# Attention with a mixture of experts on one core: when the first early expert's weights are loaded and split, and two banks at a time in its first layer

## The chip, the core and the metric

The kernel runs on one core of a Trainium2 chip. The metric is the device time of one execution in microseconds, the median of several runs. A profile is one execution recorded by the hardware profiler. The core's engines are PE (matrix products, with PEld loading their weights), DVE, ACT and POOL (vector work), and SP, whose queue issues nearly all plain transfers here.

## What is computed

Block-sparse attention over 4 batches, 8 heads, 768 tokens of width 64: in blocks of 32 tokens, each query block sees itself and its neighbours, the first and last block, and three drawn blocks; the first and last query block see all. Its output, 3072 tokens of width 512, goes through a mixture of 8 experts: a gate picks one expert for each token, and that expert's two layers are applied.

```python
scores = np.where(mask, scale * np.matmul(q, k.transpose(0, 1, 3, 2)), -1e9)
attn = softmax(scores); x = (attn @ v) as [3072, 512]
logits = x @ w_gate + modality_bias[modality_id]
e_idx = np.argmax(logits, axis=1)
for e in range(8):
    h = np.maximum(x[mask_e] @ w1[e], 0.0)        # w1[e]: 512 x 1024
    out[mask_e] = gate_w[mask_e] * (h @ w2[e])    # w2[e]: 1024 x 512
```

## The kernel before

**Attention.** The work is a list of items in a fixed order. Each pass of the main loop is one tick: it takes the next item and, for items begun some ticks earlier, the next step. The steps of a sparse item are S (scores, PE line 537), M (mask and row minimum, DVE line 545), X (exponentials, ACT line 553), T (transposes of X's result, PE line 562, in the same tick as X), A (copy of T's result out of its bank, ACT line 567), W and V (products with the values, PE lines 584 and 593), O (division, DVE lines 445 to 447), Y (transposes of the finished rows, PE line 600, copied by ACT at 602) and G (gate, PE line 610). Four items make one tile of 128 query rows. A tile's own values come through SP in six pieces of 128 KB (`fetch_own`, line 525), three at a time, and two more at lines 499 and 500; keys are picked by POOL (line 485), shared values copied by POOL (line 507), the queries loaded at line 148, finished rows stored at line 335. `hook(place)` is called at places 0 to 7 of a tick, and runs side work there: place 3 stands before the tick's S, place 7 at its end.

**Experts.** Tokens are sorted into groups of 256 that share an expert. Two groups (0 and 1) are formed early, from the experts that have enough tokens before attention is over; `early_groups` is a generator that is stepped once a tick at the place that `EARLY` gives. Group 0 belongs to the first early expert. An expert's weights are eight chunks of 512 KB: chunks 0 to 3 from w1, 4 to 7 from w2; chunks are counted on over the groups. `fetch(n)` (lines 717 and 721) has SP load chunk n into the staging buffer `staged(n)`. `split(n)` makes two halves of it: a rounded one by a cast on ACT (line 725) and the remainder by a subtraction (line 729) on DVE, or on POOL in four parts for the chunks in `POOL_SPLITS` (1, 2 and 4 among them). A staging buffer can be loaded again when both halves are made. `load(nf, ns)` fetches and splits in turn until chunk nf is fetched and chunk ns split. Its calls in the attention ticks are set by a counter of ticks:

```python
p = sum(tick >= x for x in TICKS)      # TICKS = (6, 9, 12)
load(p + 2, p)
```

So chunks 0 and 1 are fetched at the counter's tick 0, and at ticks 6, 9 and 12 one is split and another fetched into the buffer that this frees. `tail[0]` turns true some ticks after the last item has begun; then `expert_slots` takes over further buffers, and the first layer of group 0 begins.

**First layer.** `up(g, c, f, o)` (lines 777 to 779) makes three products of chunk c into column part f of a bank; two parts f fill a bank, and a bank needs all four chunks. `relu` (ACT line 784, DVE line 785) takes a full bank out. Each `yield` lets remaining attention and routing steps in between. The second layer is `down` (lines 792 to 794), fed by chunks 4 to 7. `column` (PE line 766, ACT 770, DVE 771) turns gathered tokens. After the two early groups, all other groups follow with PE near its limit.

Every engine works in the order in which the code issues to it, so what is issued earlier on an engine or a queue stands ahead of what comes later, and holds it back while it waits.

Of the kernel before, what the change touches and what calls it, by code (L numbers as in the profile page):

```python
# [62 lines left out]
LHS = (6, 5)  # L63
LHS_DVE = (True, True)
CHOOSE = ((0, 2),)
EARLY = ((3, 3),)

KL = (0, 3)
QP = (-2, 2)
# [10 lines left out]
EVAC_DVE = ()  # L80
POOL_SPLITS = (1, 2, 4, 7, 15, 16, 21)

TICKS = (6, 9, 12)
DOWN0 = ((9, 5), (9, 7), (14, 7), (12, 9), (13, 9), (13, 9), (17, 9), (15, 10))
UP1 = ((13, 8), (13, 14), (17, 15), (20, 15))
DOWN1 = ((16, 17), (17, 16), (17, 17), (23, 18), (21, 17), (23, 18), (23, 19), (22, 19))
# [3 lines left out]
def attention_moe(ctx, tc, kD, qD, qH, v0, v1, blocks, modality, w_gate, bias, w1, w2, out):  # L90
# [33 lines left out]
    with ExitStack() as actx:  # L124
# [5 lines left out]
        def bank():  # L130
            return psum.tile([P, 512], F32, name="bank")
# [522 lines left out]
        stg, wh, wl, xg, xh, xl, hh, hl, og, xq = [], [], [], [], [], [], [], [], [], []  # L654
# [41 lines left out]
        NSTG, NRING, LOOK_D, LOOK_S = 5, 5, 6, 4  # L696
# [7 lines left out]
            return experts[g]  # L704

        def staged(n):
            return stg[(0, 1, 0, 1, 0, 1, 0, 2)[n] if n < 8 else n % NSTG]

        def fetch(n):
            g, c = divmod(n, 8)  # L710
            e = expert(g)
            if c < 4:
                if g < FIRST_Q:
                    src = w1[bass.ds(e, 1), c * P:(c + 1) * P, :].rearrange("e p f -> p (e f)")
                else:
                    src = w1[bass.ds(e, 1)].rearrange("e (p c) f -> c p (e f)", c=4)[c]
                nc.sync.dma_start(staged(n), src)
            else:
                c -= 4
                src = w2[bass.ds(e, 1), 2 * c * P:(2 * c + 2) * P, :].rearrange("e (k p) f -> p (e k) f", p=P)  # L720
                nc.sync.dma_start(staged(n).rearrange("p (k f) -> p k f", k=2), src)

        def split(n, eng=None):
            h, l = wh[n % NRING], wl[n % NRING]
            nc.scalar.copy(h, staged(n))  # L725
            eng = eng or (nc.gpsimd if n in POOL_SPLITS else nc.vector)
            size = 256 if eng is nc.gpsimd else 1024
            for k in range(0, 1024, size):
                eng.tensor_tensor(l[:, k:k + size], staged(n)[:, k:k + size], h[:, k:k + size].bitcast(F32), ALU.subtract)  # L729

        def gather(g):
            ix = gi_e[g] if g < NEAR else gi[:, 2 * g:2 * g + 2]
            for t in range(2):
                nc.gpsimd.indirect_dma_start(
                    out=xg[2 * (g % 2) + t], out_offset=None, in_=x_d[0:TES[g] * P] if g < NEAR else x_d,
                    in_offset=bass.IndirectOffsetOnAxis(ap=ix[:, t:t + 1], axis=0))
# [26 lines left out]
        def column(g, n, xp):  # L763
            for c in range(2):
                for t in range(2):
                    nc.tensor.transpose(xp[:, c * GT + t * P:c * GT + (t + 1) * P],
                                        xg[2 * (g % 2) + t][:, (2 * n + c) * P:(2 * n + c + 1) * P], ident)
            h = xh[g % 2][:, 2 * n:2 * n + 2, :].rearrange("p a b -> p (a b)")
            l = xl[g % 2][:, 2 * n:2 * n + 2, :].rearrange("p a b -> p (a b)")
            nc.scalar.copy(h, xp)  # L770
            nc.vector.tensor_tensor(l, xp, h.bitcast(F32), ALU.subtract)

        def up(g, c, f, o):
            h, l = wh[(8 * g + c) % NRING], wl[(8 * g + c) % NRING]
            o = o[:, (f % 2) * GT:(f % 2 + 1) * GT]
            fs = slice(f * P, (f + 1) * P)
            nc.tensor.matmul(o, lhsT=h[:, fs], rhs=xh[g % 2][:, c, :], start=c == 0 and f % 2 == 0, stop=False)  # L777
            nc.tensor.matmul(o, lhsT=h[:, fs], rhs=xl[g % 2][:, c, :], start=False, stop=False)  # L778
            nc.tensor.matmul(o, lhsT=l[:, fs], rhs=xh[g % 2][:, c, :], start=False, stop=c == 3 and f % 2 == 1)  # L779

        def relu(k, o):
            rh = hh[0][:, 2 * k:2 * k + 2, :].rearrange("p a b -> p (a b)")
            rl = hl[k // 2][:, k % 2 * 2:k % 2 * 2 + 2, :].rearrange("p a b -> p (a b)")
            nc.scalar.activation(rh, o, AF.Relu)  # L784
            nc.vector.scalar_tensor_tensor(rl, o, 0.0, rh.bitcast(F32), ALU.max, ALU.subtract)  # L785
# [18 lines left out]
        def early_groups():  # L804
            now = {"fetch": 0, "split": 0, "gather": 0, "column": 0}

            def load(nf, ns):
                while True:
                    f, p = now["fetch"], now["split"]
                    if p < ns and p < f:  # L810
                        split(p)
                        now["split"] += 1
                    elif f < nf and f - NSTG < p and (f < 8 * NEAR or known):
                        fetch(f)
                        now["fetch"] += 1
                    else:
                        return

            def rows(g):
                if now["gather"] == g and ready[g] and (g != 1 or tail[1]):  # L820
                    if g == 1:
                        expert_slots(8)
                    gather(g)
                    now["gather"] += 1

            def columns(g):
                for n in range(2):
                    if now["column"] == 2 * g + n and now["gather"] > g:
                        column(g, n, bank())
                        now["column"] += 1  # L830
                        return

            expert_slots(0)
            tick, wait = 0, 0
            while not tail[0]:
                rows(0)
                if now["gather"]:
                    wait += 1
                    if wait > 4:
                        columns(0)  # L840
                p = sum(tick >= x for x in TICKS)
                load(p + 2, p)
                tick += 1
                yield "tick"
            expert_slots(2, 5, 6, 7)
            while now["column"] < 2:
                rows(0)
                columns(0)
            load(10, 5)
            for k in range(4):  # L850
                o = bank()
                for c in range(4):
                    for f in (2 * k, 2 * k + 1):
                        up(0, c, f, o)
                    rows(1)
                    yield
                relu(k, o)
            o = [bank() for _ in range(2)]
            for f in range(8):
                load(*DOWN0[f])  # L860
                for t in range(2):
                    down(0, f, t, o[t])
                    rows(1)
                    yield
                if f in (3, 7):
                    columns(1)
            while not tail[1]:
                yield
            rows(1)
            for t in range(2):  # L870
                give(0, t, o[t])
            while now["column"] < 4:
                columns(1)
            o = [bank() for _ in range(4)]
            for c in range(4):
                load(*UP1[c])
                for f in range(8):
                    up(1, c, f, o[f // 2])
                    if f % 2:
                        rows(2)  # L880
                        yield
            for k in range(4):
                relu(k, o[k])
            o = [bank() for _ in range(2)]
            for f in range(8):
                load(*DOWN1[f])
                for t in range(2):
                    down(1, f, t, o[t])
                    rows(2)
                    yield  # L890
                if f in (5, 6):
                    columns(2)
            for t in range(2):
                give(1, t, o[t])
            while not ready[2]:
                yield
            rows(2)
            load(22, 17)
            while now["column"] < 6:
                columns(2)  # L900
            piece_numbers(bank())
            load(22, 20)
# [128 lines left out]
        def choose(i):  # L1031
# [19 lines left out]
            if i == 0:  # L1051
                early.append(early_groups())
# [140 lines left out]
        for k, it in enumerate(sparse[0] + sparse[1]):  # L1193
            items.append(it)
            if k in DENSE_AFTER:
                c = 2 * DENSE_AFTER.index(k)
# [8 lines left out]
        def hook(place):  # L1205
            for f in work_at.pop((t, place), []):
                f()
            if t < NI:
# [4 lines left out]
                for at_, k in CHOOSE:  # L1213
                    if place == at_:
                        step(choosers, k)
                for at_, k in EARLY:
                    if place == at_:
# [124 lines left out]
        with man:  # L1342
            constants()
            for token in START:
                op, at_ = token[0], tuple(int(c) for c in token[1:] if c.isdigit())
# [13 lines left out]
            while t < NI + LAG["s"]["G"] + 1 or fillers or slots_todo or choosers or early:  # L1359
                spot = 0  # L1360
                for op in ORDER:
# [3 lines left out]
                    for kind in "ds":  # L1365
                        k = t - LAG[kind][op]
# [71 lines left out]
```

## Time and profile before

| what | value |
| --- | --- |
| median of 3 runs (lowest, highest) | 521.04 us (518.64, 523.14) |
| the profiled execution | 523.0 us |
| its span, first to last instruction | 521.2 us |
| PE busy | 497.8 us, 96% |
| DVE, ACT, POOL busy | 387.3, 339.9, 301.3 us |
| mean granted TensorE clock | 0.989 |
| transfers | 119.40 MB, mean 229 GB/s |

Times in the rows count from the span's start. 1.8 us of the profiled execution lie outside its span. PE busy at 96% leaves 23 us in which it stood; the attention's end, about 187 to 229 us, holds a large part of them. There the profile is read in order of time: what PE waited for, what that engine was doing, and what stood ahead of it in the queues.

### The profile page before, as it was taken

How to read it: one execution, taken by the hardware profiler on the slowest of the kernel's cores; microseconds unless marked ns; L12 is line 12 of the kernel's file. 1: busy time of each engine (PE TensorE's matmuls, PEld its weight loads, DVE VectorE, ACT ScalarE, POOL GpSimd, SP SyncE). 2: the span in 40 equal slices, each digit the busy share in tenths (PEclk: the TensorE clock that was granted, in tenths of full speed). 3: DMA queues.
4: the chain of work that ended last, by engine and by line, in shares of the span. 5: the costliest groups of instructions: out<-in, count | busy, mean ns of one | idle time of the engine just before them, and what ended most of it. 6: DMA issues, size and time to landing. Idle time of an engine off the chain costs nothing.

```text
span 521.2 us, 18868 instructions
## 1 busy us (share of the span) xinstructions
PE 497.8 (96%) x7170; PEld 418.5 (80%) x7170; DVE 387.3 (74%) x1125; ACT 339.9 (65%) x777; POOL 301.3 (58%) x534
## 2 busy tenths in 40 slices
PE   7999989999999997889999999999999999999993
PEld 5677776777777775788898898989979899898982
DVE  7986687687789797976975849586685867758671
ACT  3799887988889885944544646465465545645471
POOL 3579675576568874741556824473845648466313
PEclk9999999999999997999999999999999999999998
DMA  7997997778946679557767974876849677596750
GB/s 280 319 244 219 264 253 214 232 205 241 255 153 201 197 230 258 155 181 243 272 228 272 318 256 137 297 216 232 281 152 324 185 246 263 173 322 182 258 182 23
DMA packets 49698, 119.40 MB, mean 229 GB/s; under 512 B 8512, under 2 KB 8896, under 8 KB 49600
## 3 DMA queue, kind: packets, MB, share of 16 engines
q1 hardware_dynamic: 44656, 105.00, 65.2%
q0 software_dynamic: 4944, 13.11, 6.9%
q8 instruction: 58, 0.95, 0.8%
q14 instruction: 40, 0.33, 0.2%
HBM read 105.50 MB, written 12.85 MB: 227 GB/s over the span
## 4 chain that ended last, share of the span: by engine, by line
PE 79%; DMA 7%; DVE 4%; issue 4%; POOL 2%; ACT 2%; SPq 1%; POOLq 0%; DVEq 0%; ACTq 0%
PE bank L537 8%; PE bank L562 8%; PE bank L777 8%; PE bank L779 8%; PE bank L778 8%; PE bank L794 7%; PE bank L793 7%; PE bank L792 7%; DMA slot<-x_d,gq 6%; PE bank L584 4%; PE bank L593 4%; PE bank L610 2%; PE bank L438 2%; PE bank L600 2%; PE bank L419 2%
## 5 line engine op out<-in xcount | busy, mean ns | idle before, releaser
L729 DVE TENSOR_TENSOR slot<-slot 128x1024 fp32r<-128x1024 f32 x96 | 115.2, 1229 | 40.6 <-ACT slot L725 27.4
L749 POOL DMA_INDIRECT slot<-x_d,gq x72 | 93.6, 1299 | 77.2 <-DVE slot L756 57.8
L725 ACT CAST slot<-slot 128x1024 fp32r<-128x1024 f32 x104 | 106.2, 1047 | 39.3 <-PE bank L778 16.9
L777 PE MATMUL bank<-slot 128*128 128x256 f32 x384 | 107.2, 279 | 0.0
L779 PE MATMUL bank<-slot 128*128 128x256 f32 x384 | 106.3, 277 | 0.0
L778 PE MATMUL bank<-slot 128*128 128x256 f32 x384 | 106.3, 277 | 0.0
L553 ACT ACTIVATE a<-y,mn 128x256 f32<-128x256 f32 x176 | 88.7, 513 | 3.2 <-DVE mn L545 3.0
L793 PE MATMUL bank<-slot 128*128 128x512 f32 x200 | 78.7, 393 | 1.2 <-POOL slot L729 1.2
L794 PE MATMUL bank<-slot 128*128 128x512 f32 x200 | 79.0, 395 | 0.0
L792 PE MATMUL bank<-slot 128*128 128x512 f32 x200 | 78.5, 393 | 0.4 <-ACT slot L784 0.4
L778 PEld LDWEIGHTS bank<-slot 128*128 128x128 f32 x384 | 72.3, 188 | 0.4
L777 PEld LDWEIGHTS bank<-slot 128*128 128x128 f32 x384 | 72.1, 188 | 0.6
L779 PEld LDWEIGHTS bank<-slot 128*128 128x128 f32 x384 | 72.1, 188 | 0.0
L545 DVE CUSTOM_DVE_ANT_1 y<-bank,smask 128x256 f32<-128x256 f32 x176 | 66.1, 415 | 0.3
L485 POOL COPY slot<-slot 128x128 f32 x264 | 64.1, 291 | 0.0
L567 ACT COPY at<-bank 128x512 f32<-128x512 f32 x88 | 50.8, 578 | 11.1 <-PE bank L562 7.7
L507 POOL TENSOR_SCALAR slot<-slot 32x1024 f32<-32x1024 f32 x40 | 41.8, 1046 | 25.4 <-issue 10.9
L562 PE MATMUL bank<-ident,a 128*128 128x128 f32 x352 | 52.9, 283 | 0.6 <-ACT a L409 0.5
L784 ACT ACTIVATE slot<-bank 128x512 fp32r<-128x512 f32 x48 | 27.3, 599 | 38.7 <-PE bank L779 37.3
L537 PE MATMUL bank<-slot,q_raw 64*32 64x256 f32 x1408 | 49.9, 388 | 0.0
L785 DVE SCALAR_TENSOR_TENSOR slot<-bank,slot 128x512 fp32r<-128x512 f32 x48 | 30.3, 685 | 24.3 <-ACT slot L784 24.3
L793 PEld LDWEIGHTS bank<-slot 128*128 128x128 f32 x200 | 37.6, 188 | 9.9 <-POOL slot L729 1.7
(299 smaller groups left out, 867.7 us busy)
## 6 DMA issues: line engine op xcount, KB each, us to landing
slot<-w SPq DMA_DIRECT2D x105, 512.0 KB
slot<-v SPq DMA_DIRECT2D x180, 128.0 KB
q_raw<-qH SPq DMA_DIRECT2D x22, 256.0 KB
x_d<-xr SPq DMA_DIRECT2D x22, 256.0 KB
slot<-v SPq DMA_DIRECT2D x16, 256.0 KB
slot<-kD SPq DMA_DIRECT2D x13, 256.0 KB
slot<-v SPq DMA_DIRECT2D x4, 768.0 KB
slot<-kD SPq DMA_DIRECT2D x3, 768.0 KB
```

The lines of the kernel that those rows point to most:

```text
L537: nc.tensor.matmul(sp[u][32 * pr:32 * pr + 32, b * 256:(b + 1) * 256], lhsT=q[r, b * NPAIR + pr, n, :], rhs=kv[r, s0:s0 + 8, b, pr, :], st ...
L553: nc.scalar.activation(a[:, u, :], y[:, u, :], AF.Exp, bias=mn[:, u:u + 1], scale=-1.0, accum_out=total[:, u:u + 1])
L562: nc.tensor.transpose(tp[:, k:k + P], a[:, u, c * P:(c + 1) * P], ident)
L725: nc.scalar.copy(h, staged(n))
L729: eng.tensor_tensor(l[:, k:k + size], staged(n)[:, k:k + size], h[:, k:k + size].bitcast(F32), ALU.subtract)
L749: nc.gpsimd.indirect_dma_start(out=xq[0][:, 4 * t + k, :], out_offset=None, in_=table, in_offset=bass.IndirectOffsetOnAxis(ap=gq[:, k, 2 * ...
L777: nc.tensor.matmul(o, lhsT=h[:, fs], rhs=xh[g % 2][:, c, :], start=c == 0 and f % 2 == 0, stop=False)
L778: nc.tensor.matmul(o, lhsT=h[:, fs], rhs=xl[g % 2][:, c, :], start=False, stop=False)
L779: nc.tensor.matmul(o, lhsT=l[:, fs], rhs=xh[g % 2][:, c, :], start=False, stop=c == 3 and f % 2 == 1)
L792: nc.tensor.matmul(o, lhsT=hh[0][:, f, ts_], rhs=h[:, fs], start=f == 0, stop=False)
L793: nc.tensor.matmul(o, lhsT=hh[0][:, f, ts_], rhs=l[:, fs], start=False, stop=False)
L794: nc.tensor.matmul(o, lhsT=hl[f // 4][:, f % 4, ts_], rhs=h[:, fs], start=False, stop=f == 7)
```

## The change

The early generator is stepped at place 7, the tick's end. A table `SOON` of (tick, fetched, split) takes the place of `TICKS`: chunks 0 and 1 are fetched at tick 7, chunk 2 at 9, chunk 3 at 13; chunk 0 is split at tick 9, chunk 1 at 11, chunk 2 at 15. Chunk 4 has another staging buffer, in a region that attention still uses, and is fetched after the ticks; so are 5 to 8, and only chunk 3 is split ahead of the first layer. Chunk 4 is split after the first two banks. The first layer takes two banks at a time, chunk by chunk.

```diff
-EARLY = ((3, 3),)
+EARLY = ((7, 3),)
...
-TICKS = (6, 9, 12)
+SOON = ((7, 2, 0), (9, 3, 1), (11, 3, 2), (13, 4, 2), (15, 4, 3))
...
-            return stg[(0, 1, 0, 1, 0, 1, 0, 2)[n] if n < 8 else n % NSTG]
+            return stg[(0, 1, 0, 1, 4, 0, 1, 2)[n] if n < 8 else n % NSTG]
...
-                p = sum(tick >= x for x in TICKS)
-                load(p + 2, p)
+                for at_, nf, ns in SOON:
+                    if tick >= at_:
+                        load(nf, ns)
...
-            load(10, 5)
-            for k in range(4):
-                o = bank()
+            load(9, 4)
+            for k0 in (0, 2):
+                o = [bank() for _ in range(2)]
                 for c in range(4):
-                    for f in (2 * k, 2 * k + 1):
-                        up(0, c, f, o)
-                    rows(1)
-                    yield
-                relu(k, o)
+                    for k in range(2):
+                        for f in range(2):
+                            up(0, c, 2 * (k0 + k) + f, o[k])
+                        rows(1)
+                        yield
+                for k in range(2):
+                    relu(k0 + k, o[k])
+                load(10, 5)
```

On SP, before, the expert's number (`grp_e`) and chunks 0 and 1 stand behind a query load and ahead of the six value pieces of the tile that has slot 107:

```order
L703 TENSOR_LOAD grp_e0_76 [waits DVE_49]
L703 ISA x2
L717 ISA
L717 DMA slot_5390<-w1 128x1024 [waits DMAHW7_49]
L717 ISA
L717 DMA slot_5390<-w1 128x1024 [waits DMAHW0_49]
L525 ISA
L525 DMA slot_107<-v1 32x1024 [waits DMAHW1_49]
```

On SP now, the same loads stand one tile later, behind the pieces of slot 108 and ahead of lines 499 and 500 of the next tile:

```order
L525 ISA
L525 DMA slot_108<-v1 32x1024 [waits DMAHW7_49]
L703 TENSOR_LOAD grp_e0_76 [waits DVE_49]
L703 ISA x2
L717 ISA
L717 DMA slot_5398<-w1 128x1024 [waits DMAHW0_49]
L717 ISA
L717 DMA slot_5398<-w1 128x1024 [waits DMAHW1_49]
L499 DMA slot_107<-v1 32x1024 [waits DMAHW2_49,PE_49,Pool_49]
L500 DMA slot_107<-v1 32x1024 [waits DMAHW3_49]
```

Fourteen value pieces, a query load and two stores were moved ahead of the pair.

On ACT, before, from X of tick 6 on, the casts (line 725) of chunks 0 and 1 stand inside ticks 6 and 9, between X and A:

```order
L553 ACTIVATE a,sums<-y,mn 128x256 x2
L725 CAST slot<-slot 128x1024
L567 COPY at<-bank 128x16x32
L602 COPY xT<-bank 128x512
L553 ACTIVATE a,sums<-y,mn 128x256 x2
L567 COPY at<-bank 128x16x32
L553 ACTIVATE a,sums<-y,mn 128x256 x2
L567 COPY at<-bank 128x16x32
L553 ACTIVATE a,sums<-y,mn 128x256 x2
L725 CAST slot<-slot 128x1024
L567 COPY at<-bank 128x16x32
```

On ACT now, over the same ticks, chunk 0's cast alone stands there, behind A of tick 9:

```order
L553 ACTIVATE a,sums<-y,mn 128x256 x2
L567 COPY at<-bank 128x16x32
L602 COPY xT<-bank 128x512
L553 ACTIVATE a,sums<-y,mn 128x256 x2
L567 COPY at<-bank 128x16x32
L553 ACTIVATE a,sums<-y,mn 128x256 x2
L567 COPY at<-bank 128x16x32
L553 ACTIVATE a,sums<-y,mn 128x256 x2
L567 COPY at<-bank 128x16x32
L725 CAST slot<-slot 128x1024
L306 ACTIVATE exps_86<-dl 128x2x8
```

The casts of chunks 1 and 2 follow at the ends of ticks 11 and 15.

## Rows read from the trace of the kernel before

**Rows 1.** PE's timeline, 200 to 229 us: start, us, operation, count, idle before and releaser.

```profile
200.31 0.70 PE L584 MATMUL bank<-slot,at 128*64 128x64 f32 x9 [2.88 <-issue]
...
203.69 1.96 PE L537 MATMUL bank<-slot,q_raw 64*32 64x256 f32 x32
...
208.07 1.09 PE L537 MATMUL bank<-slot,q_raw 64*32 64x256 f32 x32
...
211.57 0.60 PE L562 MATMUL bank<-ident,a 128*128 128x128 f32 x4
...
217.44 1.15 PE L584 MATMUL bank<-slot,at 128*64 128x64 f32 x30 [1.40 <-ACT at L567]
...
221.67 1.09 PE L593 MATMUL bank<-slot,at 128*32 128x64 f32 x62 [0.30 <-DMA slot<-v]
...
228.06 1.09 PE L593 MATMUL bank<-slot,at 128*32 128x64 f32 x62 [1.36 <-DMA slot<-v]
```

**Rows 2.** Four stretches: busy PE, PEld, DVE, ACT, POOL; then PEclk, DMA share, GB/s.

```profile
189.00:197.40 8.40, 8.40 (x244) 6.68 (x239) 8.00 (x44) 7.59 (x26) 6.61 (x18) 1.00 0.81 225
197.40:200.30 2.90, 0.03 (x1) 0.00 (x0) 2.90 (x6) 1.49 (x4) 2.64 (x3) 0.88 0.69 192
200.30:207.00 6.70, 6.69 (x125) 4.97 (x124) 3.23 (x22) 3.62 (x11) 1.97 (x2) 0.54 0.97 284
...
217.20:229.00 11.80, 9.86 (x273) 8.69 (x273) 9.37 (x55) 8.54 (x21) 5.57 (x8) 1.00 0.77 223
```

**Rows 3.** DMA queues, 190 to 197.4 us: packets, MB, share of packet time.

```profile
q1 hardware_dynamic: 547, 1.78, 87.1%
q14 instruction: 1, 0.01, 0.4%
```

**Rows 4.** DMA queues, 197.4 to 200 us.

```profile
q8 instruction: 1, 0.02, 3.1%
```

**Rows 5.** SP's timeline, 177 to 232 us.

```profile
178.65 0.41 SPq L148 DMA_DIRECT2D q_raw<-qH  x1
...
183.05 1.36 SPq L525 DMA_DIRECT2D slot<-v  x3
...
189.65 1.59 SPq L717 DMA_DIRECT2D slot<-w  x2
...
194.37 0.36 SPq L499 DMA_DIRECT2D slot<-v  x1
197.04 0.32 SPq L500 DMA_DIRECT2D slot<-v  x1
...
220.82 2.83 SPq L525 DMA_DIRECT2D slot<-v  x6
```

**Rows 6.** SP's waits, 185 to 200 us: total, times, longest.

```profile
SPq L500 <- DMA slot<-w: 2.3, 1, 2.3
```

**Rows 7.** ACT's timeline, 209 to 217 us, the first X of tick 10 and two casts.

```profile
209.34 1.03 ACT L725 CAST slot<-slot 128x1024 fp32r<-128x1024 f32 x1
...
210.87 0.50 ACT L553 ACTIVATE a<-y,mn 128x256 f32<-128x256 f32 x1
...
215.86 1.05 ACT L725 CAST slot<-slot 128x1024 fp32r<-128x1024 f32 x1
216.79 0.59 ACT L567 COPY at<-bank 128x512 f32<-128x512 f32 x1
```

**Rows 8.** DVE's timeline at 199 us, the remainder of chunk 0.

```profile
199.05 1.21 DVE L729 TENSOR_TENSOR slot<-slot 128x1024 fp32r<-128x1024 f32 x1
```

**Rows 9.** The chain that ended last, 214 to 230 us: start, us, what.

```profile
217.73 2.12 POOL slot L729 x3
...
219.87 0.77 SPq L721
...
223.34 4.58 DMA slot<-v
```

**Rows 10.** PE's waits, 229 to 300 us: total, times, longest.

```profile
PE bank L343 <- DVE oh L313: 0.6, 1, 0.6
```

## The prediction

> **What bounds the kernel now.** I read the span by stretches of 10 us first: PE is busy throughout but for the attention's end, 187 to 229 us. There I took PE's own timeline, since what PE loses there comes out of the end of the kernel one for one: behind 229 us its longest wait is one of 0.6 us, up to 300 us [rows 10]. PE stands four times in the stretch that the change touches: 2.88 us until 200.31 for "issue", 1.40 us until 217.44 for ACT's copy A, 0.30 and 1.36 us until 221.67 and 228.06 for value pieces [rows 1]. The granted clock is 1.00 up to 197.4 and 0.54 in the mean from 200.3 to 207, a stretch at the lower of its two levels, 1.2 GHz, that begins while PE stands [rows 2]; the same 32 products of S take 1.96 us in it and 1.09 us behind it [rows 1]. So of 6.7 us, 6.7 x 1.09 / 1.96 = 3.7 is work, and the lower clock costs some 2.9 us more if the change avoids it. Behind the idle times of 1.40 and 1.36 us the clock stayed at 1.00 [rows 2]. Sum of what is lost there: 2.88 + 2.9 + 1.40 + 0.30 + 1.36 = 8.84 us.
>
> Why does PE stand for "issue"? The DMA queues answer. From 190 to 197.4 us queue 8, which brings PE's instructions, moves nothing, while 1.78 MB of data, the two weight chunks (1 MB) among them, hold 87% of the engines' time [rows 3]; its next block moves between 197.4 and 200 [rows 4], exactly while PE does nothing [rows 2]. I take it that the block was late because of the data ahead of it, that is, because chunks 0 and 1 were issued at 189.65 [rows 5].
>
> The Trainium skill speaks against this reading: "Runtime: NRT & Kernel Launch", section "Instruction fetch mechanics", has the fetch of the next 256 instructions run beside execution, its cost mostly hidden. Rows 3 and 4 show it not hidden here, but not what it waited for. By that rule the 2.88 us would have another cause and stay; that is rival E below.
>
> The value pieces come late for another reason. The load of chunk 4 waits at 219.87 for POOL's remainder of chunk 2, and the six pieces stand behind it on SP: they are issued from 220.82 on, and the last lands 4.58 us after its issue at 223.34 [rows 5, 9].
>
> **The change part by part.**
>
> *Chunks 0 and 1 leave the place at 189.65.* Removed: the 2.88 us and the 2.9 us of low clock, 5.8 together.
>
> *They come back one tile later, and chunk 0 is wanted two ticks after its load instead of six.* SP's time for it: line 499 went at 194.37, and line 500 then stood 2.3 us for one of the chunks [rows 5, 6]. Without that it goes at once and the query load follows at about 195. In the tile before, a query load at 178.65 was followed by three pieces, two stores and three pieces up to 183.05 + 1.36 = 184.4, that is 5.8 us [rows 5]. So SP is free at about 200.8 and chunk 0 goes at about 201, a few tenths for the expert's number included. It lands, by the nearest rows, between 4.6 us (the piece at 223.34) and 7.4 us later (the later of the two chunks of before had landed at 197.04, issue 189.65) [rows 5, 9]. I take 5, near the lower end, since chunk 0 is the first of its pair: 206. Its place on ACT now is just ahead of X of tick 10. Before, that X began at 210.87 [rows 7]; 5.8 us earlier is 205.1, and the cast of 1.03 us, which stood a little earlier in the same tick, would begin at 204.0. So ACT stands 206 - 204 = 2.0 us, and PE with it: T of tick 10 began at 211.57 without idle time [rows 1], right on the heels of that X. Cost 2.0 us (ends: 1.6 at a landing of 4.6, 4.4 at 7.4). I don't add low clock here, since 2.0 lies between the 1.40 that left it alone and the 2.88 that did not, somewhat nearer to the former.
>
> A rule of the Trainium skill is against this edit: "DMA: Bandwidth & Descriptors", section "Rules for kernel authors", says to issue a transfer early and to wait for it late. The change does the reverse for chunk 0; by that rule it can only lose here, and the 2.0 us are what it loses; what it wins is not in that rule, but in rows 3 and 4.
>
> *PE's instructions beside the new burst.* The two chunks now come right behind two stores and six pieces. A block that is late again could cost from nothing to 2.88 us more. I take 0: while PE stands for chunk 0, the block has the same 2 us to arrive.
>
> *ACT between tick 9 and the last X.* Two casts stand there in both versions (chunks 1 and 2 before, 0 and 1 now); chunk 2's now comes behind the last X. The 1.40 us, in which A waits behind chunk 2's cast [rows 1, 7], I keep as they are, since the same number of casts stands among the same exponentials; it could be 0 (a cast is 1.05, and one is gone from the end), or 2.4 with chunk 0's remainder on DVE, 1.21 us [rows 8], which fell into PE's idle time before and now comes among the row minima.
>
> *Chunk 4 out of the ticks.* SP no longer waits for POOL's remainder of chunk 2 ahead of the last pieces. 0.30 + 1.36 = 1.66 us go. Next late there is chunk 3's load, behind POOL's remainder of chunk 1, which is made some four ticks ahead of the products that need the pieces. Between 0 and 1.66; I take all of it.
>
> *First layer by two banks.* The products are the same, in number and size. Chunk 3 is wanted after 36 of them instead of 18, which can only help. Two relus now stand together at the end: the casts of chunks 5 and 6 come one relu later, some 0.5 us on PE if nothing covers it; against that DVE is free of a relu while it works for line 343, whose 0.6 us of idle time may go [rows 10]. I take zero, bounds -0.6 and +0.5. Chunk 4's split is now cast during the first layer, on ACT and POOL, which have little to do there; the second layer's first product is its cover.
>
> *Sum*, on the profiled execution: 523.0 - 5.8 + 2.0 - 1.66 = 517.5 us. That execution lies 2.0 us above the median of 521.04, by idle time that differs from run to run, I suppose, so against the median the same forecast is a gain of 3.5 us, 0.7%.
>
> **The rivals.**
>
> B, nothing new waits. SP reaches chunk 0 sooner, or the ticks go slower than I reckoned, and the 2.0 us don't arise: 515.5; with the 1.40 gone too, 514.1. For it: SP's place is reckoned, not seen, and 2.0 us decide. Against it: even 4.6 us of landing is more than the two ticks of that gap.
>
> C, the clock falls once more. The wait for chunk 0 is 2.9 us or more (landing 6 us or later): 517.5 + 0.9 + 2.9 = 521.3. For it: 2.88 us did it before. Against it: that takes the landing of a transfer in the midst of the burst.
>
> D, slower. The burst meets a full queue at SP's 201 to 207 us and PE's instructions are late beside the wait for chunk 0 and not beneath it: 2.88 + 2.9 more, 517.5 + 5.8 = 523.3, and with the pieces behind the pair as late as before, 525.0. It decides where transfers behind the pair take longer than the 7.4 us of before. For it: before, the pair was issued into a queue with little ahead of it, and now six pieces and two stores (6 x 128 and 2 x 256 KB) stand there; from 200.3 to 207 the DMA share was 0.97 without the pair [rows 2]. Against it: the share there included a backlog of the pair itself.
>
> E, the idle time of 2.88 us is not owed to the transfers, and stays with its low clock: chunk 0 then lands beneath it, and only the 1.66 go: 523.0 - 1.66 = 521.3.
>
> **How the numbers follow.** Forecast 0.42, B 0.22, C 0.14, E 0.08, D 0.14. The forecast's own range is 515.5 to 520; the whole range, 513.5 to 524.5, takes in B with the 1.40 and nearly all of D. A measurement can tell about 1% from no change here, 5.2 us: faster means below 515.8, slower above 526.3. Faster: all of B and a fifth of the forecast, 0.31. Slower: the part of D in which both its terms and more chunks come late, 0.09. The same: 0.60.
>
> **What would show it.** Right: no "issue" wait of PE near 197 us and a clock of 1.00 there; the pair on SP at about 201 us; ACT idle for some 2 us for slot<-w ahead of chunk 0's cast, and T behind it; no wait of line 593 for slot<-v over 0.5 us; line 777 of the first layer beginning at about 223.6 instead of 229.1. Wrong: an "issue" wait as long as before at 197 (E) or at 203 to 208 us (D), a PEclk of 0.5 in any stretch (C, D), ACT's cast of chunk 0 without a wait (B), or PE waiting in the first layer for a remainder on DVE or POOL.

## The result, and the profile after

The changed kernel takes 528.06 us in the median of 6 runs (526.76 to 531.11), the kernel before beside it 521.09 us (518.64 to 523.37): ratio 1.0116, 95% interval 1.0076 to 1.0157, so slower by some 1.2% (the quotient of the two medians is 1.0134). Run again beside other kernels it was 1.0142 (1.0079 to 1.0206). An execution over 1.5% above the fastest of its kernel counts as slow and is left out of the ratios; the profiled executions of e1 and e6 below are of that kind. The forecast of 517.5 us and its range, up to 524.5, were wrong, and so was the direction. The profiled execution took 526.76 us, its span 525.1; by the profile 3.9 us were lost against the one read before.

PE's timeline after, from 200 us on, answers to [rows 1] (start, us, operation, count, idle time before and its releaser):

```profile
201.52 1.10 PE L593 MATMUL bank<-slot,at 128*32 128x64 f32 x58 [0.49 <-issue]
...
203.57 1.09 PE L537 MATMUL bank<-slot,q_raw 64*32 64x256 f32 x32
...
213.42 0.29 PE L577 MATMUL bank<-rexp,fold 128*32 128x8 f32 x8 [4.73 <-ACT at L567]
...
218.40 1.15 PE L584 MATMUL bank<-slot,at 128*64 128x64 f32 x30 [0.68 <-ACT at L567]
...
222.05 1.08 PE L593 MATMUL bank<-slot,at 128*32 128x64 f32 x64
...
229.36 1.98 PE L584 MATMUL bank<-slot,at 128*64 128x64 f32 x32 [4.63 <-POOL slot L507]
...
233.89 0.38 PE L777 MATMUL bank<-slot 128*128 128x256 f32 x1
```

The wait of 2.88 us for issue is gone, three short ones stand in its place (0.16, 0.48, 0.49), and the 32 products of S at 203.57 take 1.09 us, at full clock. Line 593 no longer waits for value pieces. Two new waits of 4.73 and 4.63 us cost more than all that. The first layer begins at 233.89, not at 229.1 as before, let alone at 223.6 as forecast.

The same stretches by engine, answering to [rows 2] (busy PE, PEld, DVE, ACT, POOL; then PEclk, DMA share, GB/s):

```profile
200.00:208.70 8.70, 7.69 (x194) 5.81 (x193) 4.51 (x25) 3.67 (x12) 3.05 (x3) 1.00 0.99 292
208.70:213.40 4.70, 0.00 (x0) 0.00 (x0) 3.11 (x15) 2.74 (x8) 0.00 (x0) 0.95 0.63 155
213.40:217.00 3.60, 3.58 (x83) 3.24 (x84) 3.40 (x17) 3.60 (x9) 0.60 (x1) 0.59 0.74 205
217.00:224.70 7.70, 7.02 (x183) 6.31 (x183) 5.53 (x29) 7.30 (x21) 2.65 (x5) 1.00 0.76 226
224.70:229.40 4.70, 0.07 (x4) 0.04 (x2) 3.55 (x17) 0.45 (x1) 4.53 (x7) 0.70 0.20 74
229.40:234.00 4.60, 4.60 (x109) 4.06 (x110) 0.75 (x7) 1.52 (x3) 0.70 (x1) 0.57 0.67 225
```

Each of the two waits drags a stretch of low clock behind it: means of 0.59 over 3.6 us and 0.57 over 4.6 us, at most some 3.6 x 0.41 + 4.6 x 0.43 = 3.5 us if all of it was PE's work.

**The first wait.** SP, ACT and DVE after (SP's timeline; ACT's; DVE's):

```profile
201.93 0.90 SPq L717 DMA_DIRECT2D slot<-w  x2
```

```profile
209.08 1.04 ACT L725 CAST slot<-slot 128x1024 fp32r<-128x1024 f32 x1 [3.77 <-POOL slot L507]
211.70 0.22 ACT L306 ACTIVATE exps<-dl 128x16 f32<-128x16 f32 x1 [1.58 <-DVE dl L303]
```

```profile
210.16 1.23 DVE L729 TENSOR_TENSOR slot<-slot 128x1024 fp32r<-128x1024 f32 x1 [4.71 <-ACT slot L725]
211.30 0.16 DVE L300 TENSOR_REDUCE mx<-lg 128x2 f32<-128x16 f32 x1
211.49 0.17 DVE L303 TENSOR_TENSOR dl<-lg,mx 128x16 f32<-128x16 f32 x1
```

SP issues the pair at 201.93 us, 0.9 us behind my reckoning. ACT's cast of chunk 0 begins 7.1 us later. The view puts its wait down to POOL's line 507, but that line writes the shared values, which the cast doesn't read; what the cast reads is chunk 0, and in e7 below it waits as long with those copies still to come. Then comes what I had not put into the sum: DVE's remainder of chunk 0 waits for the cast and stands ahead of line 300, so dl is late, and with it the exponential of line 306. Behind that, X of tick 10 stands on ACT, and then the copy A for which PE waits.

**The second wait.** POOL after:

```profile
224.25 2.77 POOL L729 TENSOR_TENSOR slot<-slot 128x256 fp32r<-128x256 f32 x4 [5.05 <-DMA slot<-v]
227.11 2.19 POOL L507 TENSOR_SCALAR slot<-slot 32x1024 f32<-32x1024 f32 x2
```

The first row is chunk 2's remainder, which begins when ACT's cast of 223.11 is done (the view names value pieces, which a remainder doesn't read). The copies of shared values for the last tile stand behind it and end at 229.30; PE's line 584 waits for them until 229.36. Before, the order was the same and the time was not: POOL made that remainder from 217.04 on and the copies from 219.93, and line 584 of that tile came at 224.22.

### The profile page after: what moved, and what is told of

Its sections match the earlier page's. It is cut to its first block, busy times and chain, and to the rows that moved or that the text cites. A ratio compares the mean times of both kernels' runs of the same rounds, so it can differ in the third digit from the quotient of the medians.

```text
span 525.1 us, 18871 instructions
## 1 busy us (share of the span) xinstructions
PE 497.4 (95%) x7170; PEld 419.0 (80%) x7170; DVE 387.6 (74%) x1125; ACT 339.9 (65%) x777; POOL 299.5 (57%) x534
## 4 chain that ended last, share of the span: by engine, by line
issue 15%; POOL 15%; PE 10%; DMA 10%; DVE 4%; POOLq 3%; ACT 0%; DVEq 0%
POOL slot L749 12%; DMA slot<-x_d,gq 6%; DMA out<-slot,si 4%; POOL out L799 3%; POOLq L950 3%; PE bank L777 2%; PE bank L793 1%; PE bank L779 1%; PE bank L794 1%; PE bank L792 1%; PE bank L778 1%; DVE slot L756 1%; POOL slot L729 1%; DVE slot L729 0%; POOL slot L507 0%
## 5 line engine op out<-in xcount | busy, mean ns | idle before, releaser
L784 ACT ACTIVATE slot<-bank 128x512 fp32r<-128x512 f32 x48 | 27.1, 599 | 33.5 <-PE bank L779 31.8
L785 DVE SCALAR_TENSOR_TENSOR slot<-bank,slot 128x512 fp32r<-128x512 f32 x48 | 30.3, 685 | 21.8 <-ACT slot L784 21.8
```

## The experiments

Profiles of single executions are compared by one stretch: from the 16 products of line 1084 (1088 and so on where lines have moved), near 193 us, to the first product of line 777. That leaves out what differed earlier or later; in e1 the 16 products come at 201.83 us, later than in any other, and of e1 and e6 only the time of that stretch is compared. Two executions of one kernel can differ by 3.5 us in it (35.8 and 32.3 before) or agree to a tenth (41.2 twice in the changed kernel).

| kernel | 16 products | line 777 | stretch, us | ratio to before (95%) |
| --- | --- | --- | --- | --- |
| before, as read | 193.29 | 229.08 | 35.8 | |
| before again (b1, b2) | 196.86, 196.82 | 229.19, 229.41 | 32.3, 32.6 | |
| e4, two banks alone | 196.29 | 229.33 | 33.0 | 1.0025 (0.9986 to 1.0064) |
| e9, chunk 4 alone | 193.32 | 223.66 | 30.3 | 0.9970 (0.9931 to 1.0008) |
| changed, and again (a1) | 192.73, 194.85 | 233.89, 236.07 | 41.2, 41.2 | 1.0116, 1.0142 |
| e1, POOL order | 201.83 | 237.45 | 35.6 | 1.0061 (1.0024 to 1.0098) |
| e2, fetch at tick 0 | 195.06 | 233.09 | 38.0 | 1.0108 (1.0071 to 1.0146) |
| e3, both | 193.30 | 226.25 | 33.0 | 0.9995 (0.9952 to 1.0038) |
| e5, split later | 199.17 | 235.32 | 36.2 | 1.0089 (1.0050 to 1.0129) |
| e6, pair apart | 197.23 | 231.06 | 33.8 | 0.9989 (0.9954 to 1.0024) |
| e7, e1 and POOL for chunk 0 | 192.39 | 225.87 | 33.5 | 1.0021 (0.9981 to 1.0060) |
| e8, all three repairs | 194.22 | 226.74 | 32.5 | 0.9948 (0.9910 to 0.9986) |

**e1.** Against the changed kernel:

```diff
-SOON = (..., (13, 4, 2), (15, 4, 3))
+SOON = (..., (13, 4, 2), (17, 4, 3))
```

> The changed kernel with chunk 2 split at tick 17 instead of 15, so that POOL copies the shared values of the last tile (line 507) ahead of chunk 2's remainder. Theory (POOL's order holds the last tile up): PE's wait of 4.63 us for line 507 falls to about 0.8 us, and the stretch of low clock behind it goes (4.6 us at a mean of 0.57, some 2 us): 528.06 - 3.8 - 2 = 522.3 us. Rival (line 507 waits for something else, or PE then waits for chunk 2's remainder in the first layer instead): 527 to 528 us, with a wait of about 4 us at line 584 or at lines 777 to 779.

Its median was 522.24 us, but on a chip on which the kernel before took 518.85; the ratio fell from 1.0116 to 1.0061. No wait for line 507 is left among PE's waits of 190 to 238 us:

```profile
PE bank L577 <- ACT at L567: 5.4, 1, 5.4
PE bank L610 <- issue: 0.9, 1, 0.9
```

The wait for POOL goes whole, and nothing takes its place in the first layer: from line 777 up to 300 us PE's longest wait is one of 0.5 us. e3 and e7, with the same edit, have no wait for line 507 either. The stretch is 5.6 us shorter, as the theory had it (5.8); the ratio gave back half a per cent, 2.9 us, so the size is less sure than the cause.

**e2, e3.** e2 fetches the pair at tick 0, e3 does that and e1's edit:

```diff
-SOON = ((7, 2, 0), ...
+SOON = ((0, 2, 0), ...
```

> The changed kernel with chunks 0 and 1 fetched at tick 0 instead of 7, all splits as in the changed kernel. Theory (the pair in the queue held PE's instructions in the kernel before, and chunk 0's landing holds ACT in the changed one): ACT's wait of 3.77 us ahead of chunk 0's cast goes, and a wait of PE for issue near 197 us of 2 to 3 us comes back, with low clock behind it: 528.06 - 7.4 + 5.8 = 526.5 us. Rival (the issue wait of before was not owed to the pair): no such wait, PE keeps 1.00 there, 520.7 to 521.8 us.

> Both edits: chunks 0 and 1 fetched at tick 0, chunk 2 split at tick 17. If the two losses of the changed kernel are separate, the two gains add. By the theory 526.5 - 5.8 = 520.7 us, near the kernel before; by the rival on the issue wait 515 us.

PE's waits in e2, 190 to 238 us:

```profile
PE bank L584 <- POOL slot L507: 4.6, 1, 4.6
PE bank L577 <- ACT at L567: 1.9, 1, 1.9
PE bank L584 <- issue: 0.6, 1, 0.6
```

ACT's cast of chunk 0 in e2:

```profile
207.03 1.04 ACT L725 CAST slot<-slot 128x1024 fp32r<-128x1024 f32 x1
```

ACT now casts chunk 0 without a wait, so it was the landing that held it. But with the pair back in its old place the wait for issue is 0.6 us, not 2 to 3: here my theory fell, at least in size. The rival was right about that wait and wrong about the time, for 1.9 us of waiting ahead of line 577 and the 4.6 for POOL remained. By the ratio alone e2 can't be told from the changed kernel; by the stretch it is 3.2 us shorter, which is no more than executions of the kernel before differ by. e3 is at the level of the kernel before, 0.9995: as far as its interval can tell, the two losses together are the whole slowdown.

**b1, b2, a1.** The kernel before twice more, one execution each, and the changed one.

> The kernel before, profiled once more. Theory (the issue wait of 2.88 us and the low clock behind it belong to the one execution that I read, not to the kernel): PE's longest issue wait between 190 and 206 us is under 1 us, the clock stays at 1.00 there, and from the 16 products of line 1084 at 193 us to the first product of line 777 it takes about 33 us instead of 35.8. Rival (every execution has it): a wait of 2 to 3 us, low clock, 35 to 36 us.

> The kernel before, profiled a third time. Theory (the issue wait of 2.88 us is rare): PE's longest issue wait between 190 and 206 us under 1 us, 32 to 33.5 us from line 1084 to line 777. Rival (it comes in about half of the executions): 2 to 3 us and low clock, 35 to 36 us.

> The changed kernel again, beside the others on one chip. Theory (its losses are in the kernel and not in one execution): PE waits of 4 to 5 us each ahead of line 577 and of line 584 for line 507, about 41 us from the 16 products of line 1088 to the first of line 777, ratio to the kernel before 1.008 to 1.015. Rival (they vary from execution to execution as the issue wait of before did): one of the two waits under 2 us.

PE's waits in b1, then in b2, then in a1:

```profile
PE bank L584 <- ACT at L567: 1.5, 1, 1.5
PE bank L584 <- issue: 0.5, 1, 0.5
PE bank L593 <- issue: 0.3, 1, 0.3
...
PE bank L593 <- DMA slot<-v: 0.2, 1, 0.2
```

```profile
PE bank L584 <- issue: 1.7, 1, 1.7
PE bank L584 <- ACT at L567: 1.4, 1, 1.4
PE bank L610 <- issue: 1.0, 1, 1.0
```

```profile
PE bank L577 <- ACT at L567: 6.0, 2, 5.7
PE bank L584 <- POOL slot L507: 4.6, 1, 4.6
PE bank L584 <- issue: 0.5, 1, 0.5
```

The wait of 2.88 us is one execution's: 0.5 in b1, 1.7 in b2 (over my bound of 1, with the clock at 0.76 from 200 to 205), 0.29 to 0.50 in e4, which has the same loads. The stretch is 32.3 to 33.0 us in these three. Low clock is not the read execution's alone: behind the wait for copy A, 1.48 us in b1 and 1.33 in e4, the granted clock is 0.50 for 3.3 us (218.6 to 221.9 and 217.3 to 220.6), while behind the 1.40 us of the execution read it stayed at 1.00. The changed kernel's two waits came again, at 5.7 and 4.6 us, and so did its stretch, to a tenth.

**e4, e9.** Parts of the change alone, in the kernel before: the first layer by two banks as in the diff (e4), and chunk 4's other buffer, its fetch behind the ticks and its split behind the first bank (e9, whose edit stands here):

```diff
-            return stg[(0, 1, 0, 1, 0, 1, 0, 2)[n] ...
+            return stg[(0, 1, 0, 1, 4, 0, 1, 2)[n] ...
...
-                load(p + 2, p)
+                load(min(p + 2, 4), p)
...
-            load(10, 5)
+            load(9, 4)
...
                 relu(k, o)
+                load(10, 5)
```

> The kernel before with only the first layer of the first early group changed to two banks at a time; loads and splits as before. Theory (the order of the first layer is worth nothing by itself): 521.1 us, within 0.6 us, line 777 beginning at the same place. Rival (relus that stand together hold the second layer up, or a part of the slowdown is the first layer's): 522 to 524 us, with PE waits at lines 792 to 794.

> The kernel before with one part of the change alone: chunk 4 has the other staging buffer, is fetched after the ticks and split after the first bank. Theory (what the prediction counted, 1.66 us, is at most what other executions wait there, 0.23 and 1.05 us): no wait of line 593 for slot<-v over 0.3 us, ratio 0.997 to 1.000. Rival (it is all there in each execution): 0.995 to 0.997.

e4 can't be told from the kernel before. e9 is on the faster side, with an interval that reaches 1.0008, so the gain isn't settled; its wait for slot<-v was 0.6 us, not under 0.3. Its stretch of 30.3 us is the shortest of all.

**e5, e6.** The changed kernel with e1's edit and chunks 0 and 1 split two ticks later (e5); e3 with the pair fetched apart (e6):

```diff
-SOON = ((7, 2, 0), (9, 3, 1), (11, 3, 2), (13, 4, 2), (15, 4, 3))
+SOON = ((7, 2, 0), (11, 3, 1), (13, 4, 2), (17, 4, 3))                              # e5
+SOON = ((0, 1, 0), (4, 2, 0), (9, 3, 1), (11, 3, 2), (13, 4, 2), (17, 4, 3))       # e6
```

> The changed kernel with chunk 2 split at tick 17, and chunk 0 split at tick 11 and chunk 1 at 13 instead of 9 and 11; chunks 0 and 1 still fetched at tick 7. Theory (only chunk 0's landing, 5.4 to 7.1 us after its issue, holds ACT): four ticks of 1.9 us cover it, ACT's wait of 3.3 to 3.8 us ahead of the first cast falls under 1 us, and the time comes to that of fetching at tick 0, ratio to the kernel before 0.995 to 1.003. Rival (the pair's place in the queue does the harm, through PE's instructions or the value pieces behind it): ratio 1.005 or more, with issue waits or waits for slot<-v near 205 to 215 us.

> The kernel with both repairs (fetch at tick 0, chunk 2 split at tick 17), with chunk 0 fetched at tick 0 and chunk 1 at tick 4, so that the queue never takes two chunks at once. Theory (what the pair costs in the kernel before is its burst): ratio to the kernel before 0.990 to 0.997. Rival (the burst costs little in most executions): the same as with the pair, 0.997 to 1.003.

PE's longest waits in e5:

```profile
PE bank L600 <- DVE xr L447: 2.0, 1, 2.0
PE bank L1088 <- DVE hoh L1078: 1.9, 1, 1.9
PE bank L584 <- ACT at L567: 1.3, 1, 1.3
```

Neither expectation of e5 holds whole: the wait ahead of line 577 is gone, as the theory said, and the time is not; the ratio is the rival's, but the longest waits are neither for the queue nor for PE's instructions but for DVE, later, where the delayed splits now fall, with a clock of 0.50 from 230 to 235 us. POOL's steps stand one behind the other there, from 223.32 to 231.93 us, and beside them a small step of DVE, 0.16 us in the changed kernel, takes 3.09:

```profile
227.39 3.09 DVE L364 TENSOR_SCALAR r<-r 128x2 int32<-128x2 int32 x1
```

The division of line 447, for which PE waits 2.0 us, stands behind it. Splitting later moves the loss. e6 came out like e3: taking the pair apart gains nothing that can be measured, as its rival said.

**e7, e8.** Chunk 0's remainder on POOL, on top of e1 (e7) and of e3 (e8):

```diff
-POOL_SPLITS = (1, 2, 4, 7, 15, 16, 21)
+POOL_SPLITS = (0, 1, 2, 4, 7, 15, 16, 21)
```

> The changed kernel with chunk 2 split at tick 17 and chunk 0's remainder made by POOL instead of DVE, where it stands ahead of the gate's maximum (line 300) and so of the exponential at line 306, behind which ACT's row of exponentials waits. Theory (DVE's remainder adds 1.2 to 1.6 us to the wait for chunk 0): PE's wait ahead of line 577, 5.4 us with chunk 2 split at tick 17 alone, falls to about 4 us, ratio 1.002 to 1.005. Rival (ACT waits for the landing alone, or POOL's copies of line 507 come late in their turn): the wait stays above 5 us or one at line 584 takes its place, ratio 1.006 or more.

> The changed kernel with all three repairs: chunks 0 and 1 fetched at tick 0, chunk 2 split at tick 17, chunk 0's remainder on POOL. With two of them the ratio was 0.9995. Theory (DVE's remainder holds the exponentials up even where chunk 0 has landed): 1 to 2 us less, ratio 0.994 to 0.998, PE's wait ahead of line 577 of 1.5 to 2.0 us with two repairs gone. Rival (POOL's part mattered only beside the late landing): 0.998 to 1.002.

PE's longest wait in e7, then ACT's timeline there:

```profile
PE bank L577 <- DVE mn L545: 2.7, 1, 2.7
```

```profile
208.52 1.04 ACT L725 CAST slot<-slot 128x1024 fp32r<-128x1024 f32 x1 [3.78 <-issue]
209.47 0.21 ACT L306 ACTIVATE exps<-dl 128x16 f32<-128x16 f32 x1
```

ACT waits for chunk 0 as long as in the changed kernel, 3.78 us, though POOL's copies of line 507 come only at 212.71 here. But line 306 follows the cast at once, and PE's wait falls to 2.7 us, from 5.4 in e1 and 4.7 and 5.7 in the changed kernel: further than to the 4 that I expected. So DVE's remainder, ahead of the gate's row on an engine in order, was about half of the first loss. e8 beats both kernels: 0.9948, interval 0.9910 to 0.9986, beside the kernel before on one chip. As its theory had it, the wait ahead of line 577 is gone; PE's longest waits in it are for issue:

```profile
PE bank L584 <- issue: 1.9, 1, 1.9
PE bank L537 <- issue: 1.3, 1, 1.3
```

## Why the prediction was wrong

- *"Removed: the 2.88 us and the 2.9 us of low clock, 5.8 together."* The term that the forecast's gain rested on. In the changed kernel's profile the wait is gone, but most of it is gone in other executions of the kernel before too: 35.8 us of stretch against 32.3, 32.6 and 33.0, so some 3 us of the 5.8 were not the kernel's. The rows were read rightly; that they spoke for the kernel was assumed. I had allowed 2.0 us for idle time that differs from run to run, by starting from the profiled execution, and that was some 1 us too little.
- *The sign* came from chunk 0 and from POOL, both below. By the forecast the stretch was to fall from 35.8 to 30.3 us, and it rose to 41.2. With their low clock, reckoned at its most, the two new waits make up 10.9 us, about as much as that miss: 4.73 + 1.5 in the place of 2.0, and 4.63 + 2.0 in the place of nothing.
- Why PE waited for issue, the traces show further than [rows 3, 4]. Queue 8 moves 58 blocks of 16 KB in each execution, and PE has some 14516 records (products, weight loads and semaphores), so some 250 to a block. From 20 us on, the 14 profiled executions have 26 waits for issue of 0.75 us or more, and every one ends behind 1985, 2241, 3009, 8897, 9409, 9921, 10177 or 10689 records, whole multiples of 256 apart. In none of the executions did PE begin such 256 records less than 1.2 us after their block had landed. The 2.88 us ended behind 9409 records, 1.6 us after a block had landed (198.74), and that block had begun to move 4.7 us after PE began the 256 records ahead of it. With the pair at this place this took 2.0 to 3.6 us in b1, b2, e2, e3, e4, e8 and e9; with the pair later or apart (changed, a1, e1, e5, e6, e7) 0.8 to 1.9. So the pair did hold that block back, as I took it, but in those seven by little more than PE could bear: its wait there was 0 to 1.7 us. e8's 1.3 and 1.9 us are late blocks too, begun to move 4.8 and 3.7 us after.
- The rule that I set aside, of the Trainium skill, "Runtime: NRT & Kernel Launch", section "Instruction fetch mechanics", has the cost of the fetch mostly hidden. The traces agree for most blocks: PE reached all but 6 to 13 of 54 in an execution over 1.7 us after they had landed. Rival E, by which the wait was not owed to the transfers, has the blocks' times against it.
- *Chunk 0, "cost 2.0 us (ends: 1.6 and 4.4)".* The mechanism came, at 4.73 us (5.7 in a1) and with low clock behind it, which I had left out for a wait of 2.0. Two sizes were off. The cast began 7.1 us after the issue, near the upper end of 7.4, not the 5 taken. And DVE's remainder was priced as work among the row minima, up to 1 us, not as a link of the chain from chunk 0 to X of tick 10; e7 shows it worth half of the wait. The rule on early issue (the Trainium skill, "DMA: Bandwidth & Descriptors", section "Rules for kernel authors") is borne out: e2's cast has no wait.
- *Left out altogether: POOL's queue.* 4.63 us and the second low clock. Chunk 2's remainder stands ahead of the last tile's copies of line 507 in both kernels, on an engine in order; the change put its cast off by three ticks, and so the copies, from 219.93 to 227.11 us. I counted that cast on ACT alone. POOL's order showed it: now the remainders of chunks 1 and 2 stand together, ahead of the copies. e1 removes it.
- *"0.30 + 1.36 = 1.66 us go."* They went; but other executions of the kernel before lose less there (0.23 in b1, none among b2's waits, 1.05 in e4), and e9's 0.9970 doesn't exclude zero.
- *"First layer by two banks ... I take zero."* Borne out by e4.
- *The 1.40 us, kept.* 0.68 after.
- Rival D had the right sign with the wrong mechanism: no wait for issue over 0.5 us came in the burst. Rival C had the first wait: chunk 0's cast came more than 6 us after the issue, PE waited over 2.9 us, and the clock fell. Its 521.3 lacked POOL's wait and the second fall.
- Slips in the working: 6.7 less 3.7 is 3.0, not 2.9, and B with a fifth of the forecast is 0.30, not 0.31. The range was to hold nearly all of D, yet 0.09 of D's 0.14 was put above 526.3, outside it, though D's own sums end at 525.0.

## What to carry to other kernels

A wait that one profile shows is a gain only if other executions have it too: read a second profile. How far the profiled execution stands above the median does not tell: b1 and b2 stood 1.4 and 3.6 us above theirs, more or less than the 2.0 of the first, with 3 us less of stretch. When a step is moved by some ticks, list for every engine that it issues on what it now stands ahead of, and who waits for that: here a cast on ACT, a subtraction on DVE and one on POOL each stood, now later, ahead of work that PE needed next, and POOL's alone cost 4.63 us. A load that is used two ticks after its issue puts its landing on the path of the engine that reads it: here the cast came 7.1 us after the issue.

## What was not expected of the hardware

Small DVE instructions took four to six times their usual time beside a POOL copy. In e2, POOL's two copies of line 507, and DVE's two small steps in the same time:

```profile
209.40 2.17 POOL L507 TENSOR_SCALAR slot<-slot 32x1024 f32<-32x1024 f32 x2 [5.85 <-PE bank L562]
```

```profile
209.45 1.02 DVE L303 TENSOR_TENSOR dl<-lg,mx 128x16 f32<-128x16 f32 x1
210.40 0.15 DVE L1044 TENSOR_REDUCE cm<-cc 128x1 f32<-128x8 f32 x1
210.58 1.01 DVE L1047 SCALAR_TENSOR_TENSOR ce<-cc,cm,desc 128x8 f32<-128x8 f32 x1
```

In the changed kernel, with POOL idle, the first takes 0.17 us and the last 0.23. In e2 dl is on the chain to X of tick 10, so part of its 1.9 us ahead of line 577 is this. In all 14 profiled executions line 303, where a copy of line 507 stands beside it, takes 0.39 to 1.02 us and ends 0.01 to 0.03 us after a copy does; with no POOL step beside it it takes 0.16 to 0.18. e5's line 364 begins beside such a copy and ends at 230.48, 0.03 us after the third of the four parts of the remainder behind it. So beside these steps the small one ends only when one of POOL's does. No experiment here tells what ties the two engines.
